# Loading the query weights of a decode kernel in two halves, from two issuing engines

## The chip, the cores and the metric

The kernel runs on one core of a Trainium2 chip. Its time is the device time of one execution in microseconds, taken several times; the median counts. Five engines work on a core, each with its own list of instructions: TensorE (PE in the profile; PEld is its weight load), VectorE (DVE), ScalarE (ACT), GpSimd (POOL) and SyncE (SP). SP does no arithmetic here: it only issues loads and waits for semaphores. The loads are carried out by 16 DMA engines, which take their packets from a queue for each issuing engine: q1 in the profile is what SP issues, q10 what ScalarE issues.

## The reference

One token of 448 values goes through a layer norm. Two branches read the normalized row `xn`, and their results are added to `x` itself:

```python
x = A_x                                   # 1 x 1 x 448, bf16
xn = _layernorm(x, axis=-1)
return x + _A_ref(xn, A_k_cache, A_v_cache, A_wq, A_wo) \
         + _B_ref(xn, B_w_r, B_w_gate, B_w_up, B_w_down)

# A: attention with 16 query heads on 8 cached heads of 65,536 keys, 256 wide
q = xn @ wq                               # wq: 448 x 4096
p = softmax(q k^T * 256 ** -0.5)          # k_cache, v_cache: 8 x 65536 x 256
a = (p v) @ wo                            # wo: 4096 x 448
# B: a gated feed-forward with one expert, 1792 wide, scaled by sigmoid(xn . w_r)
y = (silu(xn @ w_gate) * (xn @ w_up)) @ w_down * sigmoid(xn @ w_r) + xn
```

The caches are 268 MB each, and every byte of them is read once. The query weights `wq` are 3.67 MB (3,584 KB), and the two small rows that the start needs, `x` and `w_r`, 896 bytes each.

## The kernel before, in words

**Memory.** A ring of three slots on chip, each 128 partitions of 64 KB, takes the large loads. Slots 0 and 1 take pieces of the key cache K, slot 2 pieces of the value cache V. One such piece, 8 MB or 128 rows of 64 KB, is called a turn's load; four of them (`U = 4`) make one cached head, so there are 32 for K and 32 for V. The first loads of K are cut in two halves along the row (`HALVED`), so that the work can begin on 4 MB. Before the first V, slot 2 holds the things of the start: the query weights (`wq_area`, 28 KB in each of the 128 partitions), and behind them, in partition 0, the small rows and what is made of them.

**Who issues what.** SP issues nearly all loads, in the order in which `item` appends them: first the query weights, then K for the turns 0 to 3, then the first V, and from there K and V in turn. An issue waits until TensorE has finished with the slot's former content (`FREE`, `FREEH` for a half, `VFREE`); the first V waits for the whole start, since it overwrites it. ScalarE issues two loads at the start (`act_setup`), `x` and `w_r`. These go to a row in pieces, 8 and 4, each with a small gap on chip behind it (`spaced`, `pieces`), so that one load is 8 or 4 packets. The semaphore `w0` counts both small rows; `wq` counts the query weights, and much later one of the last pieces of V.

**The start.** VectorE waits for `w0`, copies `x` to 32-bit (L373) and works out mean, variance and the normalized row (L375 to L392), with a square root on ScalarE (L410). It spreads the row into `xe_row` (L398) and then works out the product with `w_r` (L401). TensorE turns the row into columns (`XNT`), VectorE copies them (L417 to L419), and TensorE then waits for `wq` and multiplies (`QROW`). VectorE scales the result (L421), TensorE turns it (`QT`), and VectorE copies the 16 query vectors to `qT_sb` (L424). After that the first K is worked on. All of TensorE's matmuls are recorded on L433, every load on L946.

**The loop.** A turn on K takes eight sets: TensorE transposes 16 blocks (`ps_t`), VectorE and ScalarE copy them back (L495, L497), TensorE multiplies them with the query (`ps_q`) and brings the scores to their places (`ps_s`). Once the four turns of a head are done, the maximum and the exponentials follow, and from turn 4 on each turn has a block of V in its middle (`ps_o`), whose end frees slot 2. The ending does the feed-forward and the output projection between the last V loads; for the final sum it loads `x` a second time (`x_again`, two pieces, with the semaphore `wd`).

Of the kernel before, what the change touches and what calls it, by code (L numbers as in the profile page):

```python
# [7 lines left out]
ALU = mybir.AluOpType  # L8
# [14 lines left out]
def bass_parallel_sum__gqa_block_cached__moe_arch_mod__decode_kernel(  # L23
# [20 lines left out]
    P = 128  # L44
    _, Hkv, Sk, Dh = A_k_cache.shape
    D = A_x.shape[-1]
# [29 lines left out]
    SLOT = HC * CH * Dh  # L76
# [2 lines left out]
    FO = rep * NH  # L79
    WOA = (Hkv - 1) * WON  # L80
    WEN = WOA + WGN + 2 * WDN
    assert WEN + 2 * D + 8 <= SLOT
    DC = D // 4

    sb = []
# [11 lines left out]
    wo_all = slots[2][:, 0:WOA]  # L97
    wg_area = slots[2][:, WOA:WOA + WGN]
    wd_area = slots[2][:, WOA + WGN:WOA + WGN + 2 * WDN]
    def spaced(area, n):  # L100
        return area.rearrange("o (a c) -> o a c", a=n)[:, :, 0:D // n]

    def pieces(row, n):
        return row.rearrange("o (a b) -> o a b", a=n)

    XP, WP, AP_ = 8, 4, 2
    x_again = spaced(slots[2][0:1, WEN:WEN + D + 2 * AP_], AP_)
    xn_again = slots[2][0:1, WEN + D + 2 * AP_:WEN + 2 * D + 2 * AP_]
    wo_end = kt_all[:, 0:WON]
    temp = [WQN]  # L110

    def T_(n, dtype=BF16):
        n2 = n if dtype == BF16 else 2 * n
        a = slots[2][0:1, temp[0]:temp[0] + n2]
        temp[0] += n2
        assert temp[0] <= SLOT - P
        return a if dtype == BF16 else a.bitcast(dtype)
# [7 lines left out]
    sel_bf = S_("sel_bf", [P, NG, rep], BF16)  # L125
    sel2_bf = S_("sel2_bf", [P, 2, rep], BF16)
    zero_bf = S_("zero_bf", [P, 2 * rep], BF16)
    x_row = spaced(T_(D + 2 * XP), XP)
    wr_row = spaced(T_(D + 2 * WP), WP)
    xe_row = T_(2 * NE * P).rearrange("o (t r p) -> o t r p", t=2, r=NE)  # L130
    xnT_sb = S_("xnT_sb", [P, 4 * NE], BF16)
    qT_sb = S_("qT_sb", [P, NH, Hq], BF16)
# [162 lines left out]
    def v_item(t):  # L295
        slot_item("v", t, 2, None, [("VFREE", t - 1)] if t else [("QT",), ("R",), ("CONST",)])

    item("wq", [(wq_area, flat_src(A_wq, WQN), "wq")])
    for u in range(U):
        k_item(u)  # L300
    v_item(0)
# [5 lines left out]
            k_item(t + U + 1)  # L307
    slot_item("v", NT, 0, None, [("FREE", NU - 2)])
    item("wg", [(wg_area[:, 0:WGN // 2], flat_src(B_w_gate, F), "wg"), (wg_area[:, WGN // 2:WGN], flat_src(B_w_up, F), "wg")], [("VFREE", NT - 1)])
    item("wd", [(wd_area.rearrange("p (s x) -> p s x", s=2), B_w_down.rearrange("(s p t) n -> p s (t n)", s=2, p=P), "wd"), (x_again, pieces(A_x[0], AP_), "wd")])  # L310
    HL = Hkv - 2
    item("wo", [(wo_all[:, 0:HL * WON].rearrange("p (h x) -> p h x", h=HL), wo_rows(0, HL).rearrange("p h f n -> p h (f n)"), "wo"),
                (wo_all[:, HL * WON:HL * WON + WON // 2], wo_rows(HL, HL + 1)[:, 0, 0:FO // 2, :].rearrange("p f n -> p (f n)"), "wo")])
# [49 lines left out]
    def dve_setup():  # L363
        v = nc.vector
        W("dve", "z_m1p")
        O("dve", "XEZ", lambda it: v.memset(xe_row[:, :, :, :], 0.0), "sc")
        O("dve", "PSQ_ZERO", lambda it: v.memset(ps_q[:, :], 0.0), "ev0")
        O("dve", "PSO_ZERO", lambda it: v.memset(ps_o[:, :], 0.0), "ev1")
        O("dve", "s2z0", lambda it: v.memset(s2[0][:, :], 0.0), "ev2")
        O("dve", "pssz", lambda it: v.memset(ps_s[:, :], 0.0))  # L370
        O("dve", "S2Z", lambda it: v.memset(s2[1][:, :], 0.0))
        W("dve", "DMA", "w0")
        O("dve", "xf", lambda it: v.tensor_copy(out=pieces(x_f, XP), in_=x_row))  # L373
        W("dve", "xf")
        O("dve", "mean", lambda it: v.tensor_reduce(out=stat[0:1, 0:1], in_=x_f, axis=AX.X, op=ALU.add))  # L375
        W("dve", "mean")
        O("dve", "negmean", lambda it: v.tensor_scalar(out=stat[0:1, 7:8], in0=stat[0:1, 0:1], scalar1=-1.0 / D, scalar2=None,
                                                       op0=ALU.mult))
        W("dve", "negmean")
        O("dve", "xc", lambda it: v.tensor_scalar(out=xc_f, in0=x_f, scalar1=stat[0:1, 7:8], scalar2=None, op0=ALU.add))  # L380
        W("dve", "xc")
        O("dve", "sumsq", lambda it: v.tensor_tensor_reduce(out=xn_f, in0=xc_f, in1=xc_f, scale=1.0, scalar=0.0,
                                                            op0=ALU.mult, op1=ALU.add, accum_out=stat[0:1, 1:2]))
        W("dve", "sumsq")
        O("dve", "VPE", lambda it: v.tensor_scalar(out=stat[0:1, 2:3], in0=stat[0:1, 1:2], scalar1=1.0 / D, scalar2=EPS,
                                                   op0=ALU.mult, op1=ALU.add))
        W("dve", "SQRT")
        O("dve", "rstd", lambda it: v.reciprocal(out=stat[0:1, 4:5], in_=stat[0:1, 3:4]))
        W("dve", "rstd")
        O("dve", "xn", lambda it: v.tensor_scalar(out=xn_f, in0=xc_f, scalar1=stat[0:1, 4:5], scalar2=None, op0=ALU.mult))  # L390
        W("dve", "xn")
        O("dve", "XNBF", lambda it: v.tensor_copy(out=xn_bf, in_=xn_f))  # L392
        W("dve", "XNBF")
        W("dve", "XEZ")
        xv = xn_bf.rearrange("o (u s) -> o u s", s=RP)
        for t in range(2):
            e_ = xe_row[0:1, t, :, :].rearrange("o r (u t) -> o r u t", t=2)[:, :, :, t]
            O("dve", ("xe", t), lambda it, e_=e_, t=t: v.tensor_copy(  # L398
                out=e_, in_=xv[:, :, t * (NE - 1):t * (NE - 1) + NE].rearrange("o u r -> o r u")))
        alias("dve", "XE")  # L400
        O("dve", "R", lambda it: v.tensor_tensor_reduce(out=pieces(x_f, WP), in0=pieces(xn_bf, WP), in1=wr_row, scale=1.0, scalar=0.0,  # L401
                                                        op0=ALU.mult, op1=ALU.add, accum_out=stat[0:1, 5:6]))

    def act_setup():
        a = nc.scalar
        for k, (d, s, n_) in enumerate([(x_row, A_x[0], XP), (wr_row, B_w_r.rearrange("(o n) -> o n", o=1), WP)]):
            prog["act"].append(("d", here[0], ("w0", k), (d, pieces(s, n_)), "w0"))
        items["w0"] = ("w0", 32)
        W("act", "VPE")
        O("act", "SQRT", lambda it: a.activation(out=stat[0:1, 3:4], in_=stat[0:1, 2:3], func=ACTF.Sqrt), "evq")  # L410
        W("act", "R")
        O("act", "SIG", lambda it: a.activation(out=stat[0:1, 6:7], in_=stat[0:1, 5:6], func=ACTF.Sigmoid), "ev3")
        W("dve", "XNT")
        x = ps_m[0:P, C_XNT:C_XNT + 2 * NE].rearrange("p (t r) -> p r t", t=2)
        xv = xnT_sb.rearrange("p (r b t) -> p r b t", b=2, t=2)
        y, z = xv[:, :, 0, :], xv[:, 0:NE - 1, 1, :]
        O("dve", "xnt0", lambda it: nc.vector.tensor_copy(out=y, in_=x), "exp")  # L417
        O("dve", "xnt1", lambda it: nc.vector.tensor_copy(out=z[:, :, 0], in_=x[:, 1:NE, 1]))
        O("dve", "XNTSB", lambda it: nc.vector.tensor_copy(out=z[:, :, 1], in_=x[:, 0:NE - 1, 0]))  # L419
        W("dve", "QROW")  # L420
        O("dve", "QROWSB", lambda it: nc.vector.tensor_scalar(  # L421
            out=q_row[0:QROWS, :], in0=q_rows[0:QROWS, :], scalar1=inv_sqrt_dh, scalar2=None, op0=ALU.mult))
        W("dve", "QT")
        O("dve", "QTSB", lambda it: nc.vector.tensor_copy(  # L424
            out=qT_sb[:, :, :], in_=ps_m[0:P, C_Q:C_Q + NH * Hq].rearrange("p (q f) -> p f q", f=NH)), "pc", 2)
        W("act", "QTSB")
        W("act", "S2Z")
# [409 lines left out]
    def middle(T):  # L837
        pe_tot(NT)
        pe_attn()
        pe_ffn1()  # L840
        pe_ffn_hT()
        pe_ffn2()
        W_item("dve", "wd")
        O("dve", "XN_AGAIN", lambda it: nc.vector.tensor_scalar(out=pieces(xn_again, AP_), in0=x_again, scalar1=stat[0:1, 7:8], scalar2=stat[0:1, 4:5],
                                                                op0=ALU.add, op1=ALU.mult))
        W("dve", "XN_AGAIN")
        W("dve", "FFN2")
        W("dve", "ATTN")
        W("dve", "SIG")
        O("dve", "YS", lambda it: nc.vector.scalar_tensor_tensor(  # L850
            out=sum_f, in0=ps_y, scalar=stat[0:1, 6:7], in1=xn_again, op0=ALU.mult, op1=ALU.add))
        W("dve", "YS")
        O("dve", "YX", lambda it: nc.vector.tensor_tensor(out=pieces(sum_f, AP_), in0=pieces(sum_f, AP_), in1=x_again, op=ALU.add))
        W("dve", "YX")
        O("dve", "SUM", lambda it: nc.vector.tensor_tensor(out=sum_f, in0=ps_a, in1=sum_f, op=ALU.add))
        W("pe", "SUM")
        W("pe", "SCOPY", T)

        def fin_base(it):
            for g in range(NF):  # L860
                ins = mm(fin(g), lhsT=ones_f[0:1, 0:1], rhs=part(sum_f, 0, g), start=True, stop=False,
                         tile_position=(0, 32 * g), skip_group_check=True)
            return ins

        O("pe", "FIN_BASE", fin_base)
        O("pe", "OT_ZERO", lambda it: mm(ps_m[0:P, C_OT:C_OT + NH * rep], lhsT=s2[0][:, 0:P], rhs=zero_bf[:, 0:NH * rep], start=True, stop=True,
                                         skip_group_check=True))
# [313 lines left out]
```

## Time and profile before

| what | value |
|---|---|
| time, median of 3 executions | 1277.17 us (1277.15 to 1277.31) |
| the profiled execution | 1277.12 us, of it the span 1275.3 us |
| busy share: PE, DVE, ACT, POOL | 75%, 45%, 34%, 1% |
| read from HBM | 549.03 MB, 431 GB/s over the span |
| queue q1 (SP), share of 16 engines' span | 99.7% |
| queue q10 (ScalarE) | 26 packets, under 0.01 MB |
| query weights: issue, time to landing | 0.73 us, 11.6 us |
| mean granted clock of TensorE | 0.886 |

The span is the time from the first to the last instruction on the core; the device time holds a little more around it. The profile counts an engine as busy while an instruction computes, so issuing a load or waiting for a semaphore is not busy time. In a line of the order of time, the first number is the start, the second the length, both in microseconds, and the brackets at the end tell how long the engine had been idle and what ended that. SPq and ACTq are the issuing instructions of SP and ScalarE.

### The profile page before, as it was taken

What the parts mean: (1) busy time and instruction counts of PE and PEld (TensorE: products, weight loads), DVE (VectorE), ACT (ScalarE), POOL (GpSimd) and SP (SyncE); (2) the same over time, 40 slices, a digit from 0 to 9 for tenths busy, and PEclk for the clock granted to TensorE, in tenths of its full rate; (3) what the DMA queues carried; (4) which work ended last, traced back from release to release, by engine and by line L of the source; (5) the groups of instructions that cost most, each with busy time, mean ns of one, the idle gap of its engine ahead of it and who ended that gap; (6) DMA issues with size and microseconds to landing.
All of it is one profiled execution on the core that took longest, in us unless ns stands there. A gap on an engine that the chain in (4) does not pass through costs nothing.

```text
span 1275.3 us, 23430 instructions
## 1 busy us (share of the span) xinstructions
PE 955.5 (75%) x9673; PEld 622.5 (49%) x9673; DVE 570.0 (45%) x1082; ACT 436.8 (34%) x656; POOL 8.1 (1%) x38
## 2 busy tenths in 40 slices
PE   4898987778777679767678677787876797777664
PEld 2676654445544455444455444455544554444321
DVE  4665554345444455343454343453444554434310
ACT  2554433244333334323333232343332333323300
POOL 2000000000000000000000000000000000000000
PEclk9999998899888899888898887897888898888886
DMA  9999999999999999999999999999999999999998
GB/s 406 430 433 436 438 434 428 436 428 444 432 432 434 430 436 438 434 428 436 428 444 432 432 434 430 436 438 434 428 436 428 444 432 432 432 432 436 423 432 359
DMA packets 12906, 549.18 MB, mean 431 GB/s; under 512 B 1376, under 2 KB 2016, under 8 KB 3424
## 3 DMA queue, kind: packets, MB, share of 16 engines
q1 hardware_dynamic: 12870, 549.03, 99.7%
q8 instruction: 7, 0.11, 0.0%
q14 instruction: 3, 0.02, 0.0%
q10 hardware_dynamic: 26, 0.00, 0.0%
HBM read 549.03 MB, written 0.00 MB: 431 GB/s over the span
## 4 chain that ended last, share of the span: by engine, by line
DMA 77%; PE 18%; ACT 2%; issue 1%; DVE 1%; SPq 0%; ACTq 0%; DVEq 0%
DMA ring<-in_A_v_cache_dram 68%; PE ps_o L433 13%; DMA ring<-in_A_k_cache_dram 5%; PE ps_t L433 3%; DMA kt_all<-in_A_wo_dram 2%; DMA ring<-in_A_wo_dram 2%; PE ps_q L433 2%; ACT kt_all L497 2%; PE ps_m L433 1%; SPq L946 0%; DVE kt_all L495 0%; ACT S_sb L578 0%; PE ps_s L433 0%; DVE kt_all L727 0%; DVE kt_all L850 0%
## 5 line engine op out<-in xcount | busy, mean ns | idle before, releaser
L433 PE MATMUL ps_t<-ident_f,ring 128*128 128x128 f32 x4096 | 585.8, 285 | 77.6 <-DMA ring<-in_A_k_cache_dram 54.2
L495 DVE COPY kt_all<-ps_t 128x1024 bf16<-128x1024 bf16 x768 | 486.5, 684 | 285.6 <-PE ps_q L433 281.8
L433 PEld LDWEIGHTS ps_t<-ident_f,ring 128*128 128x128 f32 x4096 | 450.3, 143 | 228.9 <-issue 134.9
L497 ACT ACTIVATE kt_all<-ps_t 128x1024 bf16<-128x1024 bf16 x256 | 262.2, 1024 | 498.0 <-PE ps_q L433 497.9
L433 PE MATMUL ps_o<-ring,p_sb 128*4 128x512 bf16 x2040 | 180.4, 516 | 206.0 <-DMA ring<-in_A_v_cache_dram 201.7
L433 PEld LDWEIGHTS ps_o<-ring,p_sb 128*4 128x4 bf16 x2040 | 53.7, 103 | 295.8 <-issue 269.6
L433 PE MATMUL ps_q<-kt_all,q_cur 128*2 128x512 bf16 x2056 | 163.6, 395 | 0.3 <-DVE kt_all L495 0.3
L519 ACT ACTIVATE s<-ps_q 98x512 bf16<-98x512 f32 x257 | 151.8, 591 | 1.3 <-PE ps_q L433 1.3
L601 DVE RECIPROCAL rs<-ps_m 128x4 f32<-128x4 f32 x29 | 5.3, 182 | 275.1 <-PE ps_m L433 275.1
L588 ACT ACTIVATE p_sb<-S_sb 128x128 bf16<-128x128 bf16 x64 | 18.9, 307 | 265.6 <-PE ps_o L433 262.5
L433 PEld LDWEIGHTS ps_s<-sel_bf,s 128*128 128x128 bf16 x1032 | 64.1, 97 | 5.0 <-ACT s L519 1.9
L433 PE MATMUL ps_s<-sel_bf,s 128*128 128x8 bf16 x1032 | 63.4, 167 | 1.3 <-ACT s L519 1.3
L644 DVE CAST ob_sb<-ps_o 100x512 bf16<-100x512 f32 x29 | 20.1, 692 | 93.6 <-PE ps_o L433 93.6
L433 PEld LDWEIGHTS ps_q<-kt_all,q_cur 128*2 128x2 bf16 x2056 | 26.3, 79 | 44.5 <-issue 44.5
L433 PEld LDWEIGHTS ps_m<-rowsum,ones_f 128*128 128x128 f32 x58 | 12.4, 268 | 22.9 <-issue 22.9
L497 ACT ACT_TABLE_LOAD x7 | 9.0, 1283 | 24.2 <-PE ps_q L433 24.2
L548 DVE TENSOR_REDUCE m1p<-S_sb (+1 forms) x33 | 13.9, 422 | 4.4
L433 PE MATMUL ps_m<-rowsum,ones_f 128*128 128x4 f32 x58 | 15.0, 328 | 0.0
L546 DVE CAST S_sb<-ps_s 128x256 f32 (+1 forms) x33 | 13.6, 413 | 1.9 <-PE ps_s L433 1.9
L578 ACT ACTIVATE S_sb<-S_sb,negmax 128x512 bf16<-128x512 bf16 x16 | 13.2, 852 | 3.2 <-DVE negmax L572 3.2
L433 PE MATMUL ps_m<-diag,ones_f 2*128 2x2 f32 x58 | 11.2, 260 | 3.8 <-DVE diag L563 1.0
L433 PEld LDWEIGHTS ps_m<-diag,ones_f 2*128 2x128 f32 x58 | 8.7, 187 | 10.6 <-DVE diag L563 10.6
(96 smaller groups left out, 124.0 us busy)
## 6 DMA issues: line engine op xcount, KB each, us to landing
ring<-in_A_k_cache_dram SPq DMA_DIRECT2D x10, 4096.0 KB, 28.8
ring<-in_A_v_cache_dram SPq DMA_DIRECT2D x1, 4096.0 KB, 22.9
ring<-in_A_wq_dram SPq DMA_DIRECT2D x1, 3584.0 KB, 11.6
ring<-in_A_wo_dram SPq DMA_DIRECT2D x1, 2688.0 KB, 28.0
ring<-in_A_v_cache_dram SPq DMA_DIRECT2D x1, 2048.0 KB, 27.1
ring<-in_B_w_gate_dram SPq DMA_DIRECT2D x1, 1568.0 KB, 16.7
ring<-in_B_w_up_dram SPq DMA_DIRECT2D x1, 1568.0 KB, 20.1
ring<-in_B_w_down_dram SPq DMA_DIRECT2D x1, 1568.0 KB
```

What stands on the lines that cost most here:

```text
L433: return pe.matmul(*a, **k)
L495: O(e, ("EV", s, m), lambda it: nc.vector.tensor_copy(out=kt[:, :], in_=tb[:, :]), f"ev{m}")
L497: O(e, ("EV", s, m), lambda it: nc.scalar.activation(out=kt[:, :], in_=tb[:, :], func=ACTF.Copy), f"ev{m}")
L519: O("act", ("EVQ", s), lambda it: nc.scalar.activation(out=s2[s % 2][0:QROWS, :], in_=ps_q[0:QROWS, :], func=ACTF.Copy), "evq")
L546: O("dve", ("SCOPY", u), lambda it: nc.vector.tensor_copy(out=S_sb[:, at(it, SBN), :], in_=ps_sn), "sc")
L548: O("dve", ("SMAX", u), lambda it: nc.vector.tensor_reduce(out=m1p[:, :, at(it, 1)], in_=S_sb[:, at(it, SBN), :].rearrange("p n i -> p i n ...
L578: O("act", ("EXP", h, i), lambda it, i=i: nc.scalar.activation(out=S_sb[:, :, i], in_=S_sb[:, :, i], func=ACTF.Exp, bias=negmax[:, i:i + 1 ...
L588: O("act", ("PC", t, c), lambda it: nc.scalar.activation(out=p_sb[:, c, :, :], in_=S_sb[:, n:n + CH, :], func=ACTF.Copy), "pc")
L601: O("dve", ("RS", t), lambda it: nc.vector.reciprocal(out=rs[:, :, :], in_=ps_m[0:P, C_TOT:C_TOT + NH * rep]))
L644: O("dve", ("OB", t), lambda it: nc.vector.tensor_copy(out=ob_sb[0:OROWS, :], in_=ps_o[0:OROWS, :]))
```

## The change

The first load is now two loads of 64 partitions each: partitions 0 to 63 issued by SP, partitions 64 to 127 by ScalarE, ahead of its two small rows. Both count on `wq`, and TensorE waits for both. K follows behind SP's half. The small rows, `x` for the end among them, are now loaded whole, with no gaps, and the operations on them take whole rows.

```diff
-    x_again = spaced(slots[2][0:1, WEN:WEN + D + 2 * AP_], AP_)
-    xn_again = slots[2][0:1, WEN + D + 2 * AP_:WEN + 2 * D + 2 * AP_]
+    x_again = slots[2][0:1, WEN:WEN + D]
+    xn_again = slots[2][0:1, WEN + D:WEN + 2 * D]
...
-    x_row = spaced(T_(D + 2 * XP), XP)
-    wr_row = spaced(T_(D + 2 * WP), WP)
+    x_row = T_(D)
+    wr_row = T_(D)
...
-    item("wq", [(wq_area, flat_src(A_wq, WQN), "wq")])
+    HP = P // 2
+    item("wq", [(wq_area[0:HP, :], flat_src(A_wq, WQN)[0:HP, :], "wq")])
+    prog["act"].append(("d", here[0], ("DMA", "wq", "act"), (wq_area[HP:P, :], flat_src(A_wq, WQN)[HP:P, :]), "wq"))
+    semtot["wq"] += 16
+    items["wq"] = ("wq", semtot["wq"])
...
-        O("dve", "xf", lambda it: v.tensor_copy(out=pieces(x_f, XP), in_=x_row))
+        O("dve", "xf", lambda it: v.tensor_copy(out=x_f, in_=x_row))
...
-        for k, (d, s, n_) in enumerate([(x_row, A_x[0], XP), (wr_row, B_w_r.rearrange("(o n) -> o n", o=1), WP)]):
-            prog["act"].append(("d", here[0], ("w0", k), (d, pieces(s, n_)), "w0"))
+        for k, (d, s) in enumerate([(x_row, A_x[0]), (wr_row, B_w_r.rearrange("(o n) -> o n", o=1))]):
+            prog["act"].append(("d", here[0], ("w0", k), (d, s), "w0"))
...
-        O("dve", "XN_AGAIN", lambda it: nc.vector.tensor_scalar(out=pieces(xn_again, AP_), in0=x_again, scalar1=stat[0:1, 7:8], scalar2=stat[0:1, 4:5],
+        O("dve", "XN_AGAIN", lambda it: nc.vector.tensor_scalar(out=xn_again, in0=x_again, scalar1=stat[0:1, 7:8], scalar2=stat[0:1, 4:5],
```

The product with `w_r` (L401), the load of `x_again` and the last sums (L853) lose their pieces in the same way.

More of the change, by code (lines that the diff above doesn't have):

```diff
@@ L81, in bass_parallel_sum__gqa_block_cached__moe_arch_mod__decode_kernel @@
     WEN = WOA + WGN + 2 * WDN
-    assert WEN + 2 * D + 8 <= SLOT
+    assert WEN + 2 * D <= SLOT
     DC = D // 4
@@ L99, in bass_parallel_sum__gqa_block_cached__moe_arch_mod__decode_kernel @@
     wd_area = slots[2][:, WOA + WGN:WOA + WGN + 2 * WDN]
[L100 to L106, printed above, removed]
-    x_again = spaced(slots[2][0:1, WEN:WEN + D + 2 * AP_], AP_)
-    xn_again = slots[2][0:1, WEN + D + 2 * AP_:WEN + 2 * D + 2 * AP_]
+    x_again = slots[2][0:1, WEN:WEN + D]
+    xn_again = slots[2][0:1, WEN + D:WEN + 2 * D]
     wo_end = kt_all[:, 0:WON]
@@ L309, in bass_parallel_sum__gqa_block_cached__moe_arch_mod__decode_kernel @@
     item("wg", [(wg_area[:, 0:WGN // 2], flat_src(B_w_gate, F), "wg"), (wg_area[:, WGN // 2:WGN], flat_src(B_w_up, F), "wg")], [("VFREE", NT - 1)])
-    item("wd", [(wd_area.rearrange("p (s x) -> p s x", s=2), B_w_down.rearrange("(s p t) n -> p s (t n)", s=2, p=P), "wd"), (x_again, pieces(A_x[0], AP_), "wd")])
+    item("wd", [(wd_area.rearrange("p (s x) -> p s x", s=2), B_w_down.rearrange("(s p t) n -> p s (t n)", s=2, p=P), "wd"), (x_again, A_x[0], "wd")])
     HL = Hkv - 2
@@ L400, in dve_setup @@
         alias("dve", "XE")
-        O("dve", "R", lambda it: v.tensor_tensor_reduce(out=pieces(x_f, WP), in0=pieces(xn_bf, WP), in1=wr_row, scale=1.0, scalar=0.0,
+        O("dve", "R", lambda it: v.tensor_tensor_reduce(out=x_f, in0=xn_bf, in1=wr_row, scale=1.0, scalar=0.0,
                                                         op0=ALU.mult, op1=ALU.add, accum_out=stat[0:1, 5:6]))
@@ L852, in middle @@
         W("dve", "YS")
-        O("dve", "YX", lambda it: nc.vector.tensor_tensor(out=pieces(sum_f, AP_), in0=pieces(sum_f, AP_), in1=x_again, op=ALU.add))
+        O("dve", "YX", lambda it: nc.vector.tensor_tensor(out=sum_f, in0=sum_f, in1=x_again, op=ALU.add))
         W("dve", "YX")
```

## The prediction

> **What bounds the kernel now.** I read the DMA rows of the page first, since the kernel streams 549 MB through a chip that computes little with them. The two rows in 40 slices are the busy share and the rate; the queue row gives packets, MB and share of the 16 engines' time; the last is the issue of the query weights with its time to landing.
>
> ```profile
> DMA  9999999999999999999999999999999999999998
> GB/s 406 430 433 436 438 434 428 436 428 444 432 432 434 430 436 438 434 428 436 428 444 432 432 434 430 436 438 434 428 436 428 444 432 432 432 432 436 423 432 359
> ...
> q1 hardware_dynamic: 12870, 549.03, 99.7%
> ...
> ring<-in_A_wq_dram SPq DMA_DIRECT2D x1, 3584.0 KB, 11.6
> ```
>
> The queue that SP fills (q1) is busy 99.7% of the span, at 428 to 444 GB/s in all but the edge slices. The trace's records of single packets say it more sharply: the first large packet starts at 1.75 us, the last ends at 1272.5 us, and until 1270.6 all 16 DMA engines have one running at practically every moment. So the time is a start of 1.75 us, the bytes at a fixed rate, and a tail of 2.8 us (1275.3 - 1272.5). The profiled execution took 1277.12 us, 1.8 outside its span, against a median of 1277.17; a sum made on it needs 0.05 more to stand beside the median. TensorE, 75% busy, follows the queue. An edit can then move the time in two ways only: it changes how fast bytes flow in the stretch that it touches, or it makes SP so late with an issue that the queue runs empty.
>
> So I read the start next, in order of time (start, length, instruction, then the idle time before it and what ended that):
>
> ```profile
> 0.73 1.26 ACTq L946 DMA_DIRECT2D ring<-in_A_x_dram  x1
> 0.73 0.40 SPq L946 DMA_DIRECT2D ring<-in_A_wq_dram  x1
> ...
> 2.03 0.61 ACTq L946 DMA_DIRECT2D ring<-in_B_w_r_dram  x1
> ...
> 10.20 0.38 DVE L373 CAST ring<-ring 1x448 f32<-1x448 bf16 x1 [5.84 <-DMA ring<-in_B_w_r_dram]
> ...
> 15.60 3.16 PE L433 MATMUL ps_q<-ring,xnT_sb 128*2 128x512 bf16 x28 [0.51 <-DVE xnT_sb L419]
> ...
> 19.92 0.19 DVE L424 CAST qT_sb<-ps_m 128x32 bf16<-128x32 f32 x1 [0.42 <-PE ps_m L433]
> ...
> 22.47 1.94 PE L433 MATMUL ps_t<-ident_f,ring 128*128 128x128 f32 x8 [2.65 <-DMA ring<-in_A_k_cache_dram]
> ```
>
> To be seen: SP and ScalarE both issue at 0.73. The small rows land at 10.2, when VectorE begins the layer norm; the query vector is ready at 20.11 (19.92 + 0.19), 9.93 after the 10.18 at which the last increment of the small rows' semaphore came. The transposes of K start at 22.47 and wait for K's data, not for the query, which has 2.4 us in hand.
>
> Last, the places where SP's lead over the queue is smallest. First the order of time around 117 us, then SP's own issues:
>
> ```profile
> 116.73 0.33 SPq L946 DMA_DIRECT2D ring<-in_A_k_cache_dram  x1
> ...
> 119.97 1.09 PE L433 MATMUL ps_t<-ident_f,ring 128*128 128x128 f32 x8 [3.19 <-DMA ring<-in_A_k_cache_dram]
> ```
>
> ```profile
> 142.65 0.33 SPq L946 DMA_DIRECT2D ring<-in_A_v_cache_dram  x1
> 153.90 0.33 SPq L946 DMA_DIRECT2D ring<-in_A_k_cache_dram  x1
> ```
>
> At 119.97 TensorE has waited 3.19 us for K. The V load issued at 142.65 has its first packet run at 146.69, directly behind the K packets. Issue to first packet was 1.02 at the start (0.73 to 1.75), so that issue had 146.69 - 142.65 - 1.02 = 3.0 us to spare. A late start of TensorE is thus absorbed up to 3.2 + 3.0 = 6.2 us. The other narrow place, the K half issued at 71.09, follows packets that end from 78.9 on: 78.9 - 71.09 - 1.02 = 6.8 us. Everywhere later SP is over 10 us ahead (the next issue, at 153.90, follows a V load that lands at 166 to 168).
>
> **The change part by part.**
>
> The query weights in two halves. The bytes are the same, 128 rows of 28,672 B, 8 for each DMA engine. Before, a row took 1.062 us in the steady part (1.6 to 2.2 for the very first), which is 27.0 GB/s for an engine and 432 for 16. Each half is 64 rows, 4 for each engine if they spread as the 128 do. In before, ScalarE's packets and SP's alternate on an engine one for one: the small row's 112 B packet ran at 5.7, its semaphore write at 6.8, the next row at 7.9 to 8.6, that write at 9.0 to 9.7, always one 1.06 us packet of SP's between. So the order becomes one row for partitions 0 to 63, one for 64 to 127, on all 16 engines at the same time.
>
> No row shows what a row costs when 16 engines write into 64 partitions: every large load here covers all 128. The bounds: 1.062 us again, if only the engine limits (0 in all); and 2.124, if the receiving side is divided by partitions, half of the entries serving each half, so that two engines share one. Then a round of the first half leaves the other half's entries idle and the reverse, and the 8 rounds cost 8 x 1.062 = 8.5 us more. Two things in the trace lean to the upper end. The engine's rate does not rise when the others fall idle: 1,792 B take 0.074 us at 1269.0 with all 16 at work, and 0.074 at 1271.8, when nearly all have ended. It is no share of a common pool, so 432 GB/s is 16 separate paths, and what is left is whether they stay separate when 16 engines aim at half of the partitions. And the nearest row of several engines on one target, the 8 KB instruction fetches, goes 0.31 us alone, 0.40 by two and 0.57 in a group of four overlapping: it grows with the company. That is thin, since their target is another one; I take the upper end, less what engines gain that are out of step: the second packets start spread over 3.50 to 4.22, some 0.1 us between two that would share, which each round saves. 8 x (1.062 - 0.1) = **+7.7 us**, on the path wholly, as nothing but the queue sets the time.
>
> [...]
>
> The issue itself. SP's took 0.40 us and may take less for 64 rows: it is followed by 30 us of queued work, so nothing. ScalarE issues three loads for two: 0.4 to 1.3 us more by these rows, ahead of a table load at 2.67; its next need is the square root at 12.74, 8.8 us idle before it. Nothing, with at least 7 us of cover.
>
> The small rows behind the half on ScalarE's queue. They are now one packet each on one engine (as the output's 1x224 rows are, one of 448 B) instead of 8 and 4, and come after four rows of weights. Behind the last of those, at 11.0 + 7.7 = 18.7, each of four packets (row, semaphore, row, semaphore) waits for one K packet of 1.213: 18.7 + 4.9 + 0.45 (packet to semaphore, 9.71 to 10.18) = 24.1. The layer norm then ends the query at 24.1 + 9.9 = 34.0, and TensorE's transposes start at about 34.1 instead of 22.47: 11.6 late where the queue is 7.7 late. It loses 3.9 us of its lead, under the 6.2 that absorb it: **0**. If ScalarE's rows join two rounds later, as the small rows did (first seen at 5.7, after three rounds), two more K packets come ahead: 6.3 lost, 0.1 over; with the small rows on the latest of the engines (the last weights landed 12.31 against 11.4 for most, 0.9) another 0.9. So the upper bound is +1.0; a microsecond past the cover costs a microsecond.
>
> The rest. x again for the end is one packet instead of two, its issue (0.73 at 1182.3) no longer than before, with the queue 13 us full; the VectorE operations over pieces become whole rows: the first copy (0.38) and the reduction (0.61, behind the query's path) may go 0.1 either way; the last ones (1227 to 1232) lie under 40 us of loads that are still to land. 16 added semaphore packets of 9 ns are one for each engine. Nothing.
>
> Sum: 1277.12 + 7.7 + 0 = 1284.8, against the median 1284.9 us.
>
> **The rivals.**
>
> Not slower: the limit is the engine's alone. The halves then flow at 1.062 a row, weights land as before, the small rows at 11.0 + 4.9 + 0.45 = 16.3 instead of 10.2, TensorE starts at 26.3, 3.9 late, covered. Time 1277.2. For it: all that the packet rows show is the rate of an engine. Against: nothing in them shows engines sharing partitions without loss. It decides if a row of the weights lasts under 1.38 us (8 x 0.32 = 2.55 us, the 0.2% that I take as the least that a measurement of this kernel can tell from no change).
>
> Out of step: engines that would share an entry may be on opposite halves, when one takes SP's row and its partner ScalarE's. Each such pair loses nothing after the first rounds, but the last pair sets the landing. Half of the rounds lost gives +3.9, 1281.0. For it: starts spread by up to 0.7 us, two thirds of a row. Against: most of 16 start within 0.25 us.
>
> [...]
>
> Faster: a second queue hides the first packets' slowness (about 1.8 against 1.06): at most 0.7 us, 1276.5, no measurable gain.
>
> **How the numbers follow.** Forecast 0.64, with its own range 1283 to 1286.8 (spread of starts at one end, no spread and +1.0 of starvation at the other, rounded); out of step 0.10, of it 0.07 beyond 0.2%; not slower 0.20 and starved 0.04, both within 0.2%; faster than 0.2% 0.01; above 1286.8 0.01. Slower 0.72, same 0.27, faster 0.01. Forecast and middle leave out a quarter, so the range has to reach the unchanged case: 1277.1 to 1286.8.
>
> **What would show it.** Right: the rows of weights last about 2 us each in the packet records, the weights land 18 to 20 us after the start, slice 1 of the GB/s row falls from 406 to near 300, all later slices stand; the layer norm's first copy starts near 24, the K transposes near 34; the V issue near 154 meets a queue that isn't empty. Wrong: rows of 1.06 us and weights landed near 12, with K's transposes near 26. If later slices fall too, or a gap appears near 150 us, the starved queue is at work.

## The result and the profile after

The changed kernel takes 1287.53 us (median of six executions, 1285.59 to 1289.13) against 1277.32 before (1277.15 to 1277.49): a ratio of 1.0079, 95% interval 1.0068 to 1.0090. The change costs 10.2 us. The forecast was 7.7, so the direction and the place were right and the size was not: the median lies above the upper end of the range, 1286.8.

The six executions stand in two groups, 1285.6 to 1286.2 and 1288.9 to 1289.1, where those of before differ by 0.3 us. The profiled one took 1286.16 us and belongs to the lower group.

First the page of the changed kernel: the rate in 40 slices, the two queues (packets, MB, share of the 16 engines' span) and the two issues of the weights with their size and time to landing.

```profile
GB/s 281 436 426 440 433 443 427 433 439 435 425 433 443 431 433 429 443 427 433 439 435 425 433 445 429 433 429 443 427 433 439 435 425 435 443 429 433 426 427 360
...
q1 hardware_dynamic: 12804, 547.20, 99.0%
q10 hardware_dynamic: 86, 1.84, 0.7%
...
ring<-in_A_wq_dram SPq DMA_DIRECT2D x1, 1792.0 KB, 15.9
...
ring<-in_A_wq_dram ACTq DMA_DIRECT2D x1, 1792.0 KB, 20.3
```

Only the first slice has fallen, from 406 to 281 GB/s; the other 39 stand where they stood. Half of the weights now takes longer to land (15.9 and 20.3 us) than the whole did (11.6). Of the two, the median landing of SP's half is the earlier here because the row counts landings of a shared semaphore in their order: the packet records show ScalarE's rows first on every engine (from 2.08 us on, SP's from 8.26).

How fast the bytes flow while the weights are loaded is plainest from a table by stage. The columns are the stretch, its length, the busy time of PE, PEld, DVE, ACT and POOL with the number of instructions, the granted clock, the share of the DMA engines and the rate in GB/s. A packet counts whole in the stretch in which it starts, so a share can come out above 1, and the rate of so short a stretch is off by as much. Before:

```profile
4.00:10.00 6.00, 0.00 (x0) 0.00 (x0) 0.32 (x2) 0.00 (x0) 4.74 (x11) 1.00 0.96 408
```

After:

```profile
4.00:10.00 6.00, 0.00 (x0) 0.00 (x0) 0.33 (x2) 0.00 (x0) 4.75 (x11) 1.00 1.03 215
10.00:18.00 8.00, 0.00 (x0) 0.00 (x0) 0.00 (x0) 0.00 (x0) 0.00 (x0) 1.00 1.08 229
```

The DMA engines are as busy as before (share 1.03 against 0.96) and move half (215 GB/s against 408). Where the queue ran empty, in a run below, the share fell with the rate (0.94 and 395). So each packet takes longer, and the packet records say by how much: a row of 28,672 B lasts 2.05 to 2.30 us from the second on, where nearly all lasted 1.06 to 1.09.

The start in order of time, after (start, length, instruction, idle time before it and what ended that):

```profile
0.73 0.57 SPq L943 DMA_DIRECT2D ring<-in_A_wq_dram  x1
0.73 0.55 ACTq L943 DMA_DIRECT2D ring<-in_A_wq_dram  x1
...
21.74 0.38 DVE L370 CAST ring<-ring 1x448 f32<-1x448 bf16 x1 [17.37 <-DMA ring<-in_B_w_r_dram]
...
27.14 3.16 PE L430 MATMUL ps_q<-ring,xnT_sb 128*2 128x512 bf16 x28 [0.50 <-DVE xnT_sb L416]
...
31.46 0.19 DVE L421 CAST qT_sb<-ps_m 128x32 bf16<-128x32 f32 x1 [0.42 <-PE ps_m L430]
34.01 1.94 PE L430 MATMUL ps_t<-ident_f,ring 128*128 128x128 f32 x8 [2.65 <-issue]
```

The small rows land at 21.7 instead of 10.2, and K's transposes start at 34.01 instead of 22.47. Before, 2.65 us of waiting ahead of the transposes were put down to K's data; the same 2.65 us stand here as "issue", with K's data long landed (the first K half came at 30.7). They were TensorE's own time between the query and its first transpose all along; before, the first K half had landed at 22.02, 0.45 us ahead of the transposes. So from the landing of the small rows to the first transpose it is 12.3 us in both kernels (10.18 to 22.47, 21.72 to 34.01), and not the 9.9 that the forecast reckoned with.

Where the time went can be read from the moments at which a given number of bytes had been moved, worked out from the packet records (the bytes of a packet spread evenly over its time), as the difference to before in us:

| MB moved | 3.6 | 12 | 28 | 34 | 100 | 300 | 540 | last packet |
|---|---|---|---|---|---|---|---|---|
| after, lower group (1286.16 us) | +8.0 | +8.9 | +9.0 | +9.0 | +9.0 | +9.0 | +9.0 | +9.0 |

Of the lower group's 9.0 us, 8.9 are lost by the time the first 12 MB are in, and next to nothing is lost or won later. It is made of three parts: the first packet starts at 2.08 us instead of 1.75 (+0.33); a row of the weights lasts 2.144 us on the mean instead of 1.166, eight for each engine (+7.8); the first K rows behind them last 1.46 to 2.14 us instead of 1.21 (+0.63, spread over the engines). The sum is 8.8.

### The profile page after: what moved, and what is told of

It reads as the page before. It is cut to its first block, busy times and chain, and to the rows that moved or that the text cites. A ratio compares the mean times of both kernels' runs of the same rounds, so it can differ in the third digit from the quotient of the medians.

```text
span 1284.4 us, 23430 instructions
## 1 busy us (share of the span) xinstructions
PE 948.8 (74%) x9673; PEld 618.5 (48%) x9673; DVE 569.8 (44%) x1082; ACT 436.8 (34%) x656; POOL 8.1 (1%) x38
## 3 DMA queue, kind: packets, MB, share of 16 engines
q10 hardware_dynamic: 86, 1.84, 0.7%
## 4 chain that ended last, share of the span: by engine, by line
DMA 77%; PE 18%; ACT 2%; issue 1%; DVE 1%; SPq 0%; ACTq 0%; DVEq 0%
DMA ring<-in_A_v_cache_dram 68%; PE ps_o L430 12%; DMA ring<-in_A_k_cache_dram 3%; PE ps_t L430 3%; DMA kt_all<-in_A_wo_dram 2%; DMA ring<-in_A_wo_dram 2%; PE ps_q L430 2%; ACT kt_all L494 2%; DMA ring<-in_B_w_r_dram 2%; PE ps_m L430 1%; SPq L943 0%; DVE kt_all L492 0%; ACT S_sb L575 0%; PE ps_s L430 0%; ACTq L943 0%
## 5 line engine op out<-in xcount | busy, mean ns | idle before, releaser
L430 PE MATMUL ps_t<-ident_f,ring 128*128 128x128 f32 x4096 | 583.1, 284 | 79.4 <-DMA ring<-in_A_k_cache_dram 52.6
L430 PE MATMUL ps_o<-ring,p_sb 128*4 128x512 bf16 x2040 | 177.4, 510 | 207.6 <-DMA ring<-in_A_v_cache_dram 203.3
L430 PEld LDWEIGHTS ps_q<-kt_all,q_cur 128*2 128x2 bf16 x2056 | 26.3, 79 | 44.7 <-issue 44.7
L430 PE MATMUL ps_m<-sel_bf,ring 1*128 1x1 bf16 (+1 forms) x12 | 0.6, 166 | 27.1 <-DVE ring L395 26.3
L430 PEld LDWEIGHTS ps_m<-sel_bf,ring 1*128 1x128 bf16 (+1 forms) x12 | 0.5, 100 | 28.0 <-DVE ring L395 26.3
## 6 DMA issues: line engine op xcount, KB each, us to landing
ring<-in_A_v_cache_dram SPq DMA_DIRECT2D x1, 2048.0 KB, 27.5
ring<-in_A_wq_dram SPq DMA_DIRECT2D x1, 1792.0 KB, 15.9
ring<-in_A_wq_dram ACTq DMA_DIRECT2D x1, 1792.0 KB, 20.3
```

Of the source, the lines that this page charges most:

```text
L430: return pe.matmul(*a, **k)
```

## The experiments

Two theories were to be told apart from their rivals. **Shared partitions**: 16 DMA engines that aim at one half of the partitions slow each other to half rate, whoever issues. Rivals: **two queues** (large packets of two issuing engines slow each other, wherever they go) and **late query** (the loss comes from the late small rows, through SP's late issues). The late query is also the candidate (M1) for the upper group; its rival there is M2, slower packets in some executions. Each edit is shown against the changed kernel, with `...` where lines are left out.

### The small rows alone

```diff
-    item("wq", [(wq_area[0:HP, :], flat_src(A_wq, WQN)[0:HP, :], "wq")])
-    prog["act"].append(("d", here[0], ("DMA", "wq", "act"), (wq_area[HP:P, :], flat_src(A_wq, WQN)[HP:P, :]), "wq"))
...
+    item("wq", [(wq_area, flat_src(A_wq, WQN), "wq")])
```

> Only the small rows whole; the query weights again one load of 128 partitions by SP. 'Shared partitions' and 'two queues': 1277.2 us, as before, rows of weights 1.06 us. If the whole rows cost something themselves: above 1277.5.

Measured: 1277.23 us (1276.96 to 1277.81), ratio 0.9999 (0.9990 to 1.0009). The small rows land at 7.3 us, even earlier than in pieces (10.2), and the transposes start at 22.09 instead of 22.47. Whole rows cost nothing; what they win is hidden behind K's data, for which the transposes now wait 3.87 us, and the full queue.

### Both halves through one queue

```diff
-    item("wq", [(wq_area[0:HP, :], flat_src(A_wq, WQN)[0:HP, :], "wq")])
-    prog["act"].append(("d", here[0], ("DMA", "wq", "act"), (wq_area[HP:P, :], flat_src(A_wq, WQN)[HP:P, :]), "wq"))
...
+    item("wq", [(wq_area[0:HP, :], flat_src(A_wq, WQN)[0:HP, :], "wq"), (wq_area[HP:P, :], flat_src(A_wq, WQN)[HP:P, :], "wq")])
```

> The same two halves of 64 partitions, but both issued by SP, one after the other; ScalarE issues only the small rows (whole). 'Shared partitions': 16 engines still aim at 64 partitions at a time, so rows last 2.06 to 2.25 us and the time is 1285 to 1286.5. Rival 'two queues' (large packets of two issuing engines alternating on a DMA engine slow each other, whatever the partitions): rows 1.06 us, 1277.2.

Measured: 1286.51 us (1286.29 to 1286.60), ratio 1.0071 (1.0056 to 1.0086). The stage table of this kernel:

```profile
4.00:10.00 6.00, 0.00 (x0) 0.00 (x0) 2.98 (x6) 0.00 (x0) 4.75 (x11) 1.00 1.02 210
10.00:18.00 8.00, 0.37 (x8) 0.29 (x8) 3.49 (x14) 1.69 (x3) 0.00 (x0) 1.00 1.01 211
```

The rate is halved (210 GB/s against 408 before) with a single queue at work. The rival "two queues" falls. Note also that these four executions lie within 0.3 us: with the small rows early (landed at 7.2) there is no upper group.

### Two queues, all partitions

```diff
...
+    HW = WQN // 2
+    item("wq", [(wq_area[:, 0:HW], flat_src(A_wq, WQN)[:, 0:HW], "wq")])
+    prog["act"].append(("d", here[0], ("DMA", "wq", "act"), (wq_area[:, HW:WQN], flat_src(A_wq, WQN)[:, HW:WQN]), "wq"))
```

> Two queues as in the change, but the weights are cut along the row: 128 partitions of 14,336 B by SP, the other 14,336 B of each by ScalarE. 'Shared partitions': no sharing, packets of about 0.53 us, weights landed near 12.5; the small rows still wait behind ScalarE's half and land near 16, the transposes start near 26, which is covered: 1277.2 to 1277.6. Rival 'two queues': packets of 1.0 us and more, 1285 to 1289. Rival 'late query' (the loss comes from the late small rows): over 1280 with packets of 0.53.

Measured: 1278.71 us (1277.33 to 1280.98), ratio 1.0013 (1.0004 to 1.0022). The same two queues, the same bytes for each, but every load covers 128 partitions. The stage table of this kernel:

```profile
4.00:10.00 6.00, 0.00 (x0) 0.00 (x0) 0.33 (x2) 0.00 (x0) 4.75 (x11) 1.00 1.02 434
```

The rate is 434 GB/s. The packet records show SP's and ScalarE's packets alternating one for one on every engine, 0.54 us each for 14,336 B, and the weights in place at 12.6 us. Full rate, against 215 with the halves on the same two queues: it is the partitions that a load covers. But the time isn't all back: the executions spread over 3.7 us, and what is left of the difference in the order of work is the late small rows. From the instructions of this kernel in order of time:

```profile
16.74 0.38 DVE L370 CAST ring<-ring 1x448 f32<-1x448 bf16 x1 [12.37 <-DMA ring<-in_B_w_r_dram]
...
29.01 1.51 PE L430 MATMUL ps_t<-ident_f,ring 128*128 128x128 f32 x8 [2.65 <-issue]
```

The transposes start at 29.0, not near 26 as expected (again 12.3 us behind the rows). At the narrow place, the second half of K's fourth load, SP's issue at 78.28 finds the packets ahead of it ending at 79.4: with the 1.02 us from issue to first packet, 0.1 us to spare. This execution took 1277.77 us and lost 0.7 us there by the bytes moved; of the slower ones there is no trace.

### The small rows first, with either split

Does the late query make the spread? The small rows are put ahead of ScalarE's share, once with the halves of the change, once with the split along the row:

```diff
-    prog["act"].append(("d", here[0], ("DMA", "wq", "act"), (wq_area[HP:P, :], flat_src(A_wq, WQN)[HP:P, :]), "wq"))
...
         items["w0"] = ("w0", 32)
+        HP = P // 2
+        prog["act"].append(("d", here[0], ("DMA", "wq", "act"), (wq_area[HP:P, :], flat_src(A_wq, WQN)[HP:P, :]), "wq"))
```

> The change, but ScalarE issues its two small rows ahead of its half of the weights. Theory 'shared partitions' for the lower level plus 'late query' (M1) for the upper one: rows of weights still 2.1 to 2.25 us; small rows land before 8 us, transposes start when the weights are there, near 31, SP keeps over 3 us of lead; every execution at 1285.3 to 1286.6, none near 1289. If the upper level had another cause (M2, slower rows in some executions), about half of the executions would stay near 1289.

> Weights cut along the row on two queues as in the earlier run (1277.3 to 1281.0), but the small rows ahead of ScalarE's share. 'Late query': the whole excess of that run goes, 1277.0 to 1277.6 in every execution, small rows landed before 8 us. If the two queues themselves cost the 1.4 us: 1278 to 1281 again.

Measured: the halves 1286.72 us (five executions, 1286.37 to 1286.80), ratio 1.0072 (1.0058 to 1.0086); the split along the row 1277.20 us (eleven executions, nine of them 1276.92 to 1277.77, two at 1278.8 and 1278.95), ratio 1.0001 (0.9992 to 1.0010). From the instructions of the halves, in order of time:

```profile
7.45 1.54 DVE L369 CAST ring<-ring 1x448 f32<-1x448 bf16 x1 [3.07 <-DMA ring<-in_B_w_r_dram]
...
30.99 1.97 PE L431 MATMUL ps_t<-ident_f,ring 128*128 128x128 f32 x8 [3.02 <-DMA ring<-in_A_k_cache_dram]
```

With the small rows early the transposes wait for K again, SP has 7.9 us of lead at the narrow place, and the upper group is gone: every execution stands within 0.5 us, a little above the lower group and up to 0.2 us above what was expected. With the split along the row the median is back at that of before. The two executions near 1278.9 weren't expected, and there is no trace of them; in the profiled one (1276.92 us) the transposes start at 26.7, because ScalarE's share of the weights now ends beside K's rows (in place at 19.7), with 2.2 us of lead left. So the halves cost about 9 us by their rate alone, and the late query is what comes on top: 0.8 us between this run and the median of the change, 2.4 in its upper group.

### A late query by itself

The weights are one load again, and SP, not ScalarE, issues the two small rows, behind the first half of K:

```diff
...
+        if u == 0:
+            at_k = [i for i, en in enumerate(prog["sp"]) if en[0] == "d"][1] + 1
+            prog["sp"][at_k:at_k] = [("d", here[0], ("w0", k), (d, s), "w0") for k, (d, s) in
+                                     enumerate([(x_row, A_x[0]), (wr_row, B_w_r.rearrange("(o n) -> o n", o=1))])]
...
```

> The kernel before with the weights in one load, but the two small rows (whole) are issued by SP behind the first half of K: a measured delay of the query without any sharing of partitions. Rows of weights 1.06 us. Small rows land near 22.5, 12.3 us later than before, transposes start near 32.5, 10 late. 'Late query': the narrowest place in before had 6.9 us at the second half of K's fourth load, so a gap of about 3 us opens in the queue near 79 us, and the time is 1280 to 1281.5. If a late query costs nothing (the cover is larger than worked out): 1277.2.

Measured: 1283.89 us (1282.94 to 1285.22), ratio 1.0053 (1.0038 to 1.0069). The weights come at full rate, the small rows land at 21.3 and the transposes start at 33.55, 11.1 us late. The stage from 24 to 84 us, which before ran at 431 GB/s with a DMA share of 1.00:

```profile
24.00:84.00 60.00, 49.96 (x493) 35.58 (x494) 35.09 (x66) 25.87 (x37) 0.00 (x0) 1.00 0.94 395
```

Here share and rate fall together, since the queue ran empty (idle engines for 4.1 us in all, see below). SP's issues fall behind by more than the transposes do. The first V, which SP issues directly behind the second half of K's fourth load, tells how much, before and here:

```profile
71.55 0.34 SPq L946 DMA_DIRECT2D ring<-in_A_v_cache_dram  x1
```

```profile
83.66 0.35 SPq L941 DMA_DIRECT2D ring<-in_A_v_cache_dram  x1
```

That is 12.1 us late; among others, a pause of TensorE between the two halves of K's first load lasts 2.79 us, where it lasted 2.13. Against 6.9 of lead it leaves 5.2, and by the bytes moved the queue is 5.5 us behind at 34 MB. Three issues in a row came late (the second half of K's third load and both of its fourth): the engines stood idle for 4.1 us in all, and the first packets after each pause lasted longer than 1.21, in sum 1.6 us for each engine. So the cover was worked out rightly, and the expectation of 3 us was a miss because it counted 10 us of delay instead of 12.1.

### Even and odd partitions

```diff
-    item("wq", [(wq_area[0:HP, :], flat_src(A_wq, WQN)[0:HP, :], "wq")])
+    item("wq", [(wq_area[0:P:2, :], flat_src(A_wq, WQN)[0:P:2, :], "wq")])
...
```

The odd ones are loaded by ScalarE.

> The change, but SP loads the even partitions and ScalarE the odd ones, 64 each, over all 128. If what counts is that the 64 partitions of a load lie in one half (0 to 63 or 64 to 127), nothing is shared: rows of 1.06 us, weights at 12.5, 1277.3 to 1281 (late small rows as in the split along the row). [...]

Measured: 1280.34 us (ten executions, 1277.39 to 1282.88), ratio 1.0021 (1.0012 to 1.0031). The stage table of this kernel:

```profile
4.00:10.00 6.00, 0.00 (x0) 0.00 (x0) 0.32 (x2) 0.00 (x0) 4.75 (x11) 1.00 0.98 421
```

The rate is 421 GB/s, rows last 1.06 us and the weights are in place at 12.5. So 64 partitions in a load are not slow as such: the 64 of one half are (215 GB/s, rows of 2.05 us and more). Other 64 in a row, 32 to 95 for one, were not tried.

One rival is left. A half also reads a smaller piece of DRAM, 1,792 KB in a row, and the even or the odd partitions don't. The profile before settles it: the weights `w_gate`, 1,568 KB in a row, go to all 128 partitions there, and a row of 12,544 B lasts 0.474 us, 26.5 GB/s for an engine, nearly the 27.0 of whole loads.

The 3 us over before come late, 2.1 of them between 28 and 34 MB: at the narrow place SP's issue comes as the packets run out. The late query alone doesn't explain it, since the transposes start at 27.5, earlier than in the split along the row (29.0), and yet the issue comes 52.3 us behind them, there 49.3. In this execution TensorE had about half its clock (0.51 granted) from 42.5 to 49.4 us, as it began the second half of K's first load; the mean of the stage is the third number from the end:

```profile
24.00:84.00 60.00, 52.75 (x492) 39.28 (x496) 34.83 (x59) 25.98 (x37) 0.00 (x0) 0.94 0.99 416
```

So the later issue goes together with a lower granted clock there (0.94 on the mean, 0.97 in the split along the row). Whether that makes the spread of the other executions is not shown.

### The halves alone, and the change again

Here the edit is shown against the kernel before, so all pieces of the small rows stay:

```diff
-    item("wq", [(wq_area, flat_src(A_wq, WQN), "wq")])
+    HP = P // 2
+    item("wq", [(wq_area[0:HP, :], flat_src(A_wq, WQN)[0:HP, :], "wq")])
+    prog["act"].append(("d", here[0], ("DMA", "wq", "act"), (wq_area[HP:P, :], flat_src(A_wq, WQN)[HP:P, :]), "wq"))
+    semtot["wq"] += 16
+    items["wq"] = ("wq", semtot["wq"])
```

> The halves alone: the small rows stay in 8 and 4 pieces, behind ScalarE's half. The halves carry the whole loss: rows of 2.05 to 2.25 us, 1285.5 to 1289.5, as the full change. If the whole rows had a share of it: 0.5 us or more below the full change's median of 1287.5 with the same two levels.

Measured: 1289.24 us (1288.31 to 1289.57), ratio 1.0094 (1.0077 to 1.0111). The halves carry the whole loss. All four executions are at or near the upper level: in pieces on several engines the small rows landed at 26.3, later than in any execution of the change that is listed below. The intervals of this run and of the full change overlap, so that the whole rows help within the change isn't shown beyond that.

The change itself, repeated for its upper group:

> The changed kernel, unaltered, for its two levels (three executions at 1285.6 to 1286.2 us, three at 1288.9 to 1289.1). Theory 'shared partitions' (16 engines aiming at one half of the partitions go at half rate): the rows of weights last 2.06 to 2.25 us in every execution, and the two levels come from the order in which the halves' rows meet. At the upper level one of two things must show: (M1) the small rows land later than the 21.7 us of the profile in hand, by enough that SP issues a load after the queue has run empty (a gap of about 3 us between 100 and 160 us); or (M2) no gap, but rows of K of 32 KB that last about 2.4 us instead of 1.21 beside rows of the weights, and weights that land 3 us later. A profile at the lower level should repeat: weights landed at 21.0, no gap, 1285.6 to 1286.2.

> The changed kernel unaltered, one profiled execution, to meet the upper level. 'Late query' (M1): an execution above 1288 us shows small rows landed at 25 us or later, the transposes' start at 37.5 or later, SP's issue of the second half of K's fourth load behind the end of the packets ahead of it (lead below 0), and DMA engines idle between 60 and 100 us; rows of weights last 2.05 to 2.25 us as at the lower level. An execution below 1287 shows a lead above 0 there and no idle engine. M2: above 1288 without a gap, with slower rows.

> As the look before: above 1288 us only with small rows landed at 25 us or later and a gap in the queue between 60 and 100 us (M1), or without a gap (M2).

> As the two looks before: an execution above 1288 us only with small rows landed at 25 us or later and a gap in the queue between 60 and 100 us (M1), or without a gap (M2).

Measured: 1287.51 us in the repeat with interval (five executions, 1285.89 to 1289.48, ratio 1.0083, interval 1.0070 to 1.0097), and 1286.79, 1287.47 and 1286.16 us in the three single ones. So there are executions between the two groups as well. No profiled execution of the change fell into the upper group itself; the profiled ones order like this (the lead is that of SP's issue of the second half of K's fourth load, as worked out in the prediction; no lead means that engines ran empty around 88 us):

| execution | small rows landed | transposes start | lead | time |
|---|---|---|---|---|
| after | 21.7 | 34.0 | 4.6 | 1286.16 |
| repeat with interval | 23.9 | 36.2 | 1.0 | 1286.46 |
| single repeat 3 | 26.1 | 38.4 | 0.2 | 1286.16 |
| single repeat 1 | 26.0 | 38.2 | none | 1286.79 |
| single repeat 2 | 26.0 | 38.3 | none | 1287.47 |
| halves, rows in pieces | 26.3 | 38.6 | none | 1288.31 |

From single repeat 1, the landing of the small rows and the start of the transposes:

```profile
26.04 0.38 DVE L370 CAST ring<-ring 1x448 f32<-1x448 bf16 x1 [21.68 <-DMA ring<-in_B_w_r_dram]
...
38.20 1.94 PE L430 MATMUL ps_t<-ident_f,ring 128*128 128x128 f32 x8 [2.65 <-issue]
```

The rows of weights last 2.05 to 2.14 us on the mean in all six, 2.09 in the slowest and 2.14 in one of the fastest, so M2 falls. What differs is whose rows come first on the engines: ScalarE's three times in the first line, SP's in the last four, with the small rows behind more or fewer of the others. The landing alone doesn't order the executions: single repeat 3 landed as late as 1 and 2 and kept 0.2 us of lead, since TensorE's pause between the two halves of K's first load, 2.29 and 2.16 us in those two, is missing there. Two expectations failed in part: single repeat 1 has no lead though it stands below 1287 us, and the pause of the queue is near 88 us and under 1 us long, not 3 us between 100 and 160.

Where the lead is used up the queue pauses, as the stage from 84 to 92 us shows, first of the profile after, then of the halves with pieces:

```profile
84.00:92.00 8.00, 7.74 (x84) 5.98 (x76) 6.47 (x12) 4.63 (x7) 0.00 (x0) 1.00 1.03 442
```

```profile
84.00:92.00 8.00, 7.65 (x81) 5.53 (x79) 5.08 (x9) 4.05 (x8) 0.00 (x0) 1.00 0.92 369
```

By the bytes moved, single repeat 2 and the halves with pieces are 8.5 and 8.6 us behind before at 28 MB, 9.5 at 34 MB, and as much at 540: the pause costs 0.9 to 1.0. Their last packets are behind by more, 10.4 and 11.2. The 16 engines don't end together: the last V piece lands over 1.84 us in the profile after, 2.82 in single repeat 2 and 3.56 with pieces (1.97 before), while the middle engine of the 16 is 9.4 to 9.5 us late in both. So the slow executions seen here are a pause near 88 us plus one or two engines that end late. Why these do is open; in the repeat with interval it takes 2.50 us too, without a pause. It is shown that the upper group goes with the late small rows; the full 3 us haven't been seen in a profile.

## Why the prediction was right or wrong, point by point

Of the 10.2 us at the median the halves are 7.8, as forecast. The steps that failed are terms put at nothing: the issue (+0.33), K's first rows (+0.63) and above all the small rows, where the **0** rested on 9.9 us from their landing to the transposes. Measured were 12.3, and where the rows land late that uses up the cover. The lower group, which has only the first two on top, lies inside the range; the group that has the third as well took the median out of it.

- **What bounds the kernel** held: nothing but the start changed, and in the lower group it came through to the end one for one (+8.9 at 12 MB, +9.0 at the last packet).
- **The weights in two halves**: of the two bounds the upper one was met, and the term 8 x (1.062 - 0.1) = 7.7 came within 0.1 of the measured +7.8, partly by luck. That two engines share an entry of the receiving side was the author's supposition: the runs show that the rate halves (215 GB/s against 408), not by what. The 0.1 for engines out of step was not there: all 16 run rows of the same half, round by round. Each of the seven later rows lasted 1.10 us more (2.17 against 1.07 on the mean), and the first only 0.15 (1.96 against 1.81), since a first row is slow before too. A row could also last more than twice 1.062: in the profile after, rows of the two halves in turn ran at 2.05 to 2.11, two of the same half in a row at 2.21 to 2.30. Of the two signs that leaned to the upper end, neither is strong: around 1269 us packets of 1,792 B take 0.074 to 0.088, not 0.074 throughout, and of the group of four instruction fetches two took 0.38 and 0.40, not 0.57, and no trace shows what these fetches aim at.
- **The issue itself, costed at nothing**: wrong by +0.33. An issue for 64 partitions takes SP 0.56 to 0.58 us instead of 0.39 to 0.40, and the first packet starts at 2.08 instead of 1.75; it starts at 2.08 to 2.12 in every run whose first load has 64 partitions, with one queue (2.08) and with even partitions (2.08) too.
- **K behind the weights** was costed as before; its first rows took +0.63.
- **The small rows**: forecast landed at 24.1, measured 21.7 to 26.1 by the order of the queues. The step that failed is the 9.9 us from there to the transposes. It is 12.3, because 2.65 us that the profile put down to K's data belonged to TensorE. Those 2.4 us "in hand" didn't exist, and with them the lost lead of 3.9 becomes 6.2 at 24.1, the whole of the smaller cover. In single repeat 1 the transposes start 15.7 us late where the queue is 8.4 late: 7.3 are lost, more than the 6.9 at the place that gave way. So the **0** of that part was right for the lower group and wrong for the upper one.
- **The cover** was worked out rightly at the second half of K's fourth load: a lead of 6.9 us there, and no run shows a gap at the V load near 147 us, where it was put at 6.2. Beyond the cover a late issue costs a little more than itself: 5.2 us too late cost 5.5 with the late query alone, and 0.5 to 0.6 cost 0.9 to 1.1 in the three lines of the table without lead.
- **The rivals**: "not slower" and "out of step" fell, since no row of the weights lasted under 1.38 us (1.49 at the least for a first row, 2.05 for a later one). The starved queue, which had 0.04 by itself, came together with the slow rows, and the upper group goes with it.
- **The range**: its upper end took +8.5 and +1.0. With the measured terms, +0.3, +7.8, +0.6 and up to 3 for the late query, it should have reached 1289.

No version here beats the kernel before: the queue is full from 1.75 us on (99.7% of the span), and the two at its time (whole rows; split along the row with the small rows first) only equal it.

## What to carry to other kernels

A load of partitions 0 to 63, or of 64 to 127, occupied all 16 DMA engines at half their rate here: 210 to 234 GB/s, from one queue or two, against 408 to 436 for loads over all 128. On two queues the two halves took 18.0 us from the start of their first packet to the end of their last, the weights in one load 10.1. The load cut along the row and shared between the same two queues ran at 434 GB/s, so that is the better cut. A DMA share that stays at 1 while GB/s halves (1.02 and 210) says slow packets; share and rate falling together (0.94 and 395) say an empty queue. And a small load queued behind a large one on the same queue landed with it (at 21.7 us, where issued first it was there by 7.45): when it heads a chain of dependent work, issue it first, and measure that chain to the first instruction that really starts, since a wait put down to a transfer may hide another of the same length, as the 2.65 us did here.

## What the runs showed that was not expected

- Even partitions at full rate (421 GB/s) with the same count of 64 that halves the rate when all lie in one half (210 to 234).
- TensorE's part in SP's lead: a pause of up to 2.8 us between the halves of K's first load that one execution lacks, and half its clock for 7 us in another.
- A longer issue and a later first packet for a load of 64 partitions (0.57 and 2.08 us) than for one of 128 (0.39 and 1.76).
- A small row in one packet landed sooner than in 8 and 4 pieces (7.3 against 10.2 us); that it then waits for one engine and not for the latest of several would explain it, but was not tried by itself; ScalarE's issue of `x` is shorter too (0.53 against 1.26 us).
